# A linear-attention and expert kernel on one core: both heads' transposes and k-v products put into one stretch behind the third projection tile, and TensorE's order fixed in pairs 2 to 7

## Chip, cores and metric

The kernel runs on one core of one Trainium2 chip. The metric is the device time of one execution in microseconds (us), as a median over runs. All other times here are read from one profiled execution, and are counted from the start of its span. A "matmul" below is one TensorE instruction; a product of two unrounded fp32 tiles is two of them, a transpose is one.

## What is computed

The reference has three stages, and the change is in the first: an attention with random features, for 2 batches of 8 heads, 576 tokens and a head size of 64, with 128 features.

```python
def phi(x):
    proj = np.einsum('bhsd,md->bhsm', x, omega)
    sq = np.sum(x * x, axis=-1, keepdims=True) / 2.0
    h = proj - sq
    h = h - np.max(h, axis=-1, keepdims=True)
    return np.exp(h) / np.sqrt(m)
q_p, k_p = (phi(q_s), phi(k_s))
kv = np.einsum('bhsm,bhsd->bhmd', k_p, v)
z = np.sum(k_p, axis=2)
num = np.einsum('bhsm,bhmd->bhsd', q_p, kv)
den = np.einsum('bhsm,bhm->bhs', q_p, z)[..., None] + 1e-06
```

Behind it come a dense layer pair (`g = h * tanh(softplus(h))` between `x @ w_in` and `@ w_out`), and a top-1 mixture of 8 experts.

## The kernel before

The heads are taken in eight pairs (0 to 7). The loop over `i` at lines 407 to 445 has one round for each pair and one more. In round `i` the kernel projects pair `i` and finishes the pair before it, `a = i - 1`.

**Projection.** A pair's keys and queries are cut into tiles of 128 tokens: four tiles, and a fifth in odd pairs for the last 64 tokens of this pair and of the one before. `proj(i, t)` (line 246) makes one tile: six matmuls of rounded fp32 (two calls of `mm3`, whose three matmuls stand in lines 72, 73 and 74) into one PSUM bank of the tag "pj". There are three such banks, taken in turn, so a tile waits until the tile three before it in that tag has been read for the last time. (Tile 3 of pairs 0 and 1 lies in another bank, line 251.) Below, (2,2) is tile 2 of pair 2, its third.

**Features.** `phi(i, t)` (line 261) takes a tile out of its bank: VectorE finds the maximum of each row (line 266), ScalarE takes exponentials of the two key blocks (line 273), and the two query blocks are shifted, by ScalarE in even tiles (line 276, two instructions) and by VectorE in odd ones (line 271). Until then the bank is held.

**Finishing a pair.** For head `h` of pair `a`, `qtr(a, h)` (line 314) transposes the shifted query features (four transposes, line 322) and ScalarE takes their exponential into `qT` (line 323). `kvm(a, h)` (line 278) multiplies keys with v (eight matmuls, line 285, and in odd pairs two more for the last tokens, line 287). In odd pairs `qtr(a, 2)` does the last tokens' transposes (two, line 326), and `kvc` (line 305) copies z and kv out of PSUM, on ScalarE. `ratio` (line 336) begins with `heads`, the matmuls `den` and `num` (line 334, 8 and 16 of them), which need `qT`, `z` and `kv` of two pairs: `den` and `num` of the first token half are made in the round right behind the pair that completes them.

**Order.** `beat(i, t, *pe)` projects a tile, then runs the functions in `pe`, then traces `phi`. What stands in `pe` behind tiles 1, 2, 3 and 4 is the list `extra`, line 422:

```python
q = [(lambda h=h: qtr(a, h)) for h in range(3 if a % 2 else 2)]
kv = [(lambda h=h: kvm(a, h)) for h in range(2)] + [lambda: kvc(a // 2)] * (a % 2)
...
    extra = [q[0], kv[0]], [], [q[1], *kv[1:]], q[2:]
```

So head 0 stands behind tile 1 (the second), head 1 behind tile 3 (the fourth). This part of the program goes through a list scheduler at build time. It may place the instructions of an engine in another order than they are traced in, wherever data and buffers allow; `tc.issue_after(x)` keeps what is traced inside behind x on the same engine. The order on each engine is then fixed in the program. Behind this stage the order is as written (`manual_schedule`, line 472 on).

Of the kernel before, what the change touches and what calls it, by code (L numbers as in the profile page):

```python
# [22 lines left out]
NPAIR = NB * NH // 2  # L23
# [10 lines left out]
def performer_mish_moe(  # L34
# [16 lines left out]
    T, V, S, P = nc.tensor, nc.vector, nc.scalar, nc.gpsimd  # L51
# [13 lines left out]
    def split_hi_lo(src, hi, lo, eng_hi="act", eng_lo="pool"):  # L65

        round_hi(src, hi, eng_hi)
        take_lo(src, hi, lo, eng_lo)

    def mm3(o, lh, ll, rh, rl, start, stop):  # L70

        T.matmul(out=o, lhsT=lh, rhs=rh, start=start, stop=False)  # L72
        T.matmul(out=o, lhsT=lh, rhs=rl, start=False, stop=False)  # L73
        return T.matmul(out=o, lhsT=ll, rhs=rh, start=False, stop=stop)  # L74
# [4 lines left out]
    ident = cpool.tile([128, 128], F32, name="ident")  # L79
# [18 lines left out]
    def bank(tag, name):  # L98
        return psum.tile([128, 512], F32, name=name, tag=tag, bufs={"pj": 3, "qt": 2}.get(tag, 1))

    def twin(name):

        return psum.tile([128, 2, 512], F32, name=name, tag="b12", bufs=1)
# [60 lines left out]
    def advance(*gens):  # L164

        for x in gens:
            next(x, None)

    def finish(*gens):

        for x in gens:
            for _ in x:
                pass
# [18 lines left out]
    with ExitStack() as c2:  # L192
# [14 lines left out]
        V.tensor_scalar(out=omh, in0=omf, scalar1=SCALE, scalar2=None, op0=ALU.mult)  # L207
        V.scalar_tensor_tensor(out=oml, in0=omf, scalar=SCALE, in1=omh.bitcast(F32), op0=ALU.mult, op1=ALU.subtract)
        st = {}

        def pieces(p):
            cuts = {0: (0, 256, 768, 1024), 1: (0, 512, 1280)}.get(p, (0, 1280 if p % 2 else 1024))
            return [slice(*c) for c in zip(cuts, cuts[1:])]
# [12 lines left out]
        def vload(p):  # L228
            w = 780 if p % 2 else 520
            with tc.issue_after(st[2]["load"].ins) if p == 1 else ExitStack():  # L230
                nc.sync.dma_start(out=st[p]["v"][:, 0:w], in_=va[p][:, 0:w])

        def halves(p):

            return (("act", "dve"),) * 3 if p == 0 else (("pool", "pool"),) * 2 + (("dve", "pool"),) * 2 if p == 1 else (("pool", "pool"),) * 5

        def split(p):
            d = st[p]
            d["h"] = a3.tile([128, 1280], F32R, name="kqh", tag="kqh")
            d["l"] = a3.tile([128, 1280], F32R, name="kql", tag="kql")  # L240
            cut = pieces(p)[1:] if p == 0 else [slice(0, 256), slice(256, 512), slice(512, 768), slice(768, 1280)] if p == 1 else [slice(c, c + 256) for c in range(0, 1280 if p % 2 else 1024, 256)]
            for c, e in zip(cut, halves(p)):
                split_hi_lo(d["f"][:, c], d["h"][:, c], d["l"][:, c], *e)
                yield

        def proj(p, t):
            d = st[p]

            if (p, t) == (0, 3):
                st["twin"] = twin("pj")  # L250
            d["p", t] = ps = st["twin"][:, p, :] if t == 3 and p < 2 else bank("pj", "pj")
            for i in range(2):
                s = slice(256 * t + 128 * i, 256 * t + 128 * i + 128)
                if (p, t) == (0, 0):

                    T.matmul(out=ps[:, i * 256 : i * 256 + 256], lhsT=d["f"][:, s], rhs=oms, start=True, stop=True)
                    continue
                with tc.issue_after(st[0]["mm"].ins) if p == 0 and (t, i) > (1, 0) or p == 1 and t < 2 else ExitStack():
                    st[0]["mm"] = mm3(ps[:, i * 256 : i * 256 + 256], d["h"][:, s], d["l"][:, s], omh, oml, True, True)

        def phi(p, t):

# [15 lines left out]
        def kvm(p, h):  # L278

            d, du = st[p], st[p // 2, "u"]  # L280
            if p % 2 == 0 and h == 0:
                du["K"] = bank("b0", "kvp")
            e, v, K, c = d["e"], d["v"], du["K"], (2 * h + p % 2) * 65
            for t in range(4):
                T.matmul(out=K[:, c : c + 65], lhsT=e[t][:, h, :], rhs=v[:, (2 * t + h) * 65 : (2 * t + h + 1) * 65], start=(p % 2 == 0 and h == 0 and t == 0), stop=False)  # L285
            if p % 2:
                T.matmul(out=K[:, h * 130 : h * 130 + 130], lhsT=e[4][:, h, :], rhs=v[:, 520 + h * 130 : 650 + h * 130], start=False, stop=(h == 1))

        def lead(t):

# [23 lines left out]
        def qtr(p, h):  # L314
            e, d = st[p]["e"], st[p // 2, "u"]
            if p % 2 == 0 and h == 0:
                d["qT"] = a2.tile([128, 2, 2, SEQ], F32, name="qT", tag="qT")
            qT = d["qT"]
            q = bank("qt", "qt")
            if h < 2:  # L320
                for t in range(4):
                    T.transpose(q[:, t * 128 : t * 128 + 128], e[t][:, 2 + h, :], ident)  # L322
                S.activation(out=qT[:, p % 2, h, 0:512], in_=q, func=AF.Exp)
            else:
                for i in range(2):
                    T.transpose(q[:, i * 128 : i * 128 + 128], e[4][:, 2 + i, :], ident)
                S.activation(out=qT[:, :, :, 512:SEQ], in_=q[:, 0:256].rearrange("p (h r t) -> p r h t", h=2, r=2), func=AF.Exp)

        def heads(u, o, t0, w, s):

            d, n = st[u, "u"], o.shape[-1]
            for i in range(4):
                r, h = divmod(i, 2)
                T.matmul(out=o[32 * i : 32 * i + 32, :], lhsT=d[w][:, h, r, s], rhs=d["qT"][:, r, h, t0 : t0 + n], start=True, stop=True, tile_position=(0, 32 * i))  # L334

        def ratio(u, c, last=False):

# [68 lines left out]

        for i in range(NPAIR + 1):
            a, u, odd = i - 1, (i - 3) // 2, i % 2 == 1
            sp = split(i + 2) if i + 2 < NPAIR and i > 0 else iter(())
            advance(sp)  # L410
            if i == 1:
                lead(0)
            beat(i, 0, *([lambda: ratio(u, 1 - i % 2)] if u >= 0 else []))
            if i == 0:
                with tc.issue_after(st[0]["max"].ins):
                    finish(sp0)
            q = [(lambda h=h: qtr(a, h)) for h in range(3 if a % 2 else 2)]
            kv = [(lambda h=h: kvm(a, h)) for h in range(2)] + [lambda: kvc(a // 2)] * (a % 2)
            if i < 2:
                extra = [], [], [], []  # L420
            else:
                extra = [q[0], kv[0]], [], [q[1], *kv[1:]], q[2:]
            for t in range(4):
                if i == 0 and t > 1:
                    with tc.issue_after(st[0]["max"].ins):
                        advance(sp1)
                advance(sp)
                if i == 1 and t == 0:
                    lead(1)
                beat(i, t + 1, *extra[t])  # L430
                if i == 1 and t < 2:
                    lead(t + 2)
                if i == 0 and t == 3:
                    finish(sp1, split(2))
            finish(sp)
            if i + 3 < NPAIR:
                load(i + 3)
            if i + 2 < NPAIR:
                vload(i + 2)
            if i == 2:  # L440
                with tc.issue_after(st[4]["load"].ins):
                    nc.sync.dma_start(out=cs, in_=cst)
            with tc.issue_after(st[4]["load"].ins) if i == 2 else ExitStack():
                for x in loads.get(i, ()):
                    fetch(*x)
# [26 lines left out]
    with tc.manual_schedule():  # L472
# [116 lines left out]
        for k in range(4):  # L589
            s, now = 9 * k + 6, [3 * k + 1, 3 * k + 2, 3 * k + 3]  # L590
# [272 lines left out]
        for j in range(NJ):  # L863
# [4 lines left out]
            e = "pool" if j < 5 else "act"  # L868
# [68 lines left out]
        o = y2.tile([TT, 3, DM], F32, name="o", tag="o")  # L937
# [14 lines left out]
        o = y2.tile([TT, 3, DM], F32, name="o", tag="o")  # L952
# [33 lines left out]
    with tc.If(R["nrem"] > 0, label="rest"):  # L986
        with ExitStack() as c2:
# [5 lines left out]
            with tc.For_i(0, G, 1) as gi:  # L993
                ps = [*(bank("pj", "pq") for _ in range(3)), bank("b0", "pq")]
                for j in range(NJ):
                    t = q2.tile([128, 512], I64, name="wo64", tag="wo64")
                    nc.sync.dma_start(out=t, in_=w_out[j])
                    f = q2.tile([128, 512], F32, name="wof", tag="wof")
# [5 lines left out]
            with tc.For_i(0, G, 1) as gi:  # L1004
                with tc.For_i(0, E, 1) as ei:
                    n = nc.values_load(R["cnti"][0:1, ds(gi * E + ei, 1)], min_val=0, max_val=GT, skip_runtime_bounds_check_because="a count of a group's tokens")
                    with tc.If(n > 0):
# [7 lines left out]
                        w = q1.tile([TT, 3], F32, name="w", tag="w")  # L1015
# [7 lines left out]
                        for t in range(3):  # L1023
# [3 lines left out]
                            o = ob[:, ds(gi * 3 + t, 1), :].rearrange("p o d -> p (o d)")  # L1027
# [12 lines left out]
    with tc.manual_schedule():  # L1040
        yo3.append(cpool.tile([128, 4, 4, E], F32, name="yt2", tag="us", bufs=1).rearrange("p j q e -> p (j q e)")[:, 0:TT])
        pt = [bank("pj", "pt") for _ in range(3)]
        for t in range(3):
            c = slice(t * TT, t * TT + TT)
# [71 lines left out]
```

## Time and profile before

| | |
|---|---|
| median of 3 runs | 295.41 us (294.96 to 296.36) |
| the profiled execution | 294.71 us |
| its span, first to last instruction | 293.0 us |
| TensorE matmuls busy | 287.7 us, 98% |
| VectorE, ScalarE, GpSimd busy | 73%, 65%, 25% |
| granted TensorE clock, mean | 1.000 |

The span and the profiled execution's own time differ by what lies around the span, 1.71 us. A busy matmul row overlaps the next one, so busy time tells only that TensorE had something in hand; the distance between two starts tells what an instruction costs.

### The profile page before, as it was taken

To read this page: it belongs to the slowest core of one execution; us is meant where nothing else is said; L and a number is where in the kernel's file an instruction comes from. 1 tells how busy PE (TensorE), PEld (TensorE's weight loads), DVE (VectorE), ACT (ScalarE), POOL (GpSimd) and SP (SyncE) were. 2 spreads that over 40 slices of the span, in tenths; PEclk is the share of its full clock that TensorE was granted. 3 is DMA by queue.
4 is the path that set the end of the run, shared out by engine and by line. 5 is a ranking of instruction groups with operands and counts; after the bars stand their busy time and mean duration, and the time that the engine had idled before them with its cause. 6 is when DMAs were issued, how large, how long until landed. Compare 5 with 4: busy or idle time off the path is not lost.

```text
span 293.0 us, 6011 instructions
## 1 busy us (share of the span) xinstructions
PE 287.7 (98%) x2276; PEld 269.3 (92%) x2277; DVE 215.3 (73%) x392; ACT 189.9 (65%) x374; POOL 73.2 (25%) x110
## 2 busy tenths in 40 slices
PE   8999999999999999999999999999999999999994
PEld 5998988877999999999979997879999999999994
DVE  4766667997999999999898099958647764636621
ACT  4997787975294787978966989625446554435311
POOL 3899994232021101010021176300000000000000
PEclk9999999999999999999999999999999999999999
DMA  6767731230166579954610000000345508622011
GB/s 208 251 217 287 245 110 55 74 110 35 72 218 209 161 229 314 328 162 145 220 69 0 0 2 0 3 0 3 107 141 153 176 27 271 210 72 82 1 42 46
DMA packets 18433, 37.03 MB, mean 126 GB/s; under 512 B 1632, under 2 KB 7616, under 8 KB 18400
## 3 DMA queue, kind: packets, MB, share of 16 engines
q1 hardware_dynamic: 18256, 36.47, 38.0%
q8 instruction: 19, 0.31, 0.4%
q10 hardware_dynamic: 144, 0.13, 0.2%
q14 instruction: 14, 0.11, 0.1%
HBM read 33.06 MB, written 3.54 MB: 125 GB/s over the span
## 4 chain that ended last, share of the span: by engine, by line
PE 97%; DMA 1%; DVE 0%; ACT 0%; issue 0%
PE h L72 12%; PE h L74 11%; PE h L73 11%; PE py L72 9%; PE py L73 9%; PE py L74 9%; PE kvp L285 4%; PE pj L72 3%; PE pj L74 3%; PE ph L72 3%; PE ph L73 3%; PE ph L74 3%; PE pj L73 3%; PE num L334 3%; PE lg L532 3%; PE qt L322 2%
## 5 line engine op out<-in xcount | busy, mean ns | idle before, releaser
L72 PE MATMUL h<-xh,wih 128*128 128x384 f32 x192 | 64.7, 337 | 0.0
L74 PE MATMUL h<-xh,wil 128*128 128x384 f32 x192 | 64.3, 335 | 0.0
L73 PE MATMUL h<-xl,wih 128*128 128x384 f32 x192 | 64.2, 334 | 0.0
L72 PE MATMUL py<-gh,whi 128*128 128x288 f32 x128 | 38.4, 300 | 0.0
L63 DVE TENSOR_TENSOR wl<-wl,whi 128x512 fp32r<-128x512 f32 x48 | 33.9, 712 | 5.3 <-PE py L74 3.6
L73 PE MATMUL py<-gh,whi 128*128 128x288 f32 x128 | 37.6, 294 | 0.0
L74 PE MATMUL py<-gh,wl 128*128 128x288 f32 x128 | 37.5, 293 | 0.0
L72 PEld LDWEIGHTS h<-xh,wih 128*128 128x128 f32 x192 | 36.0, 188 | 1.1 <-issue 1.1
L73 PEld LDWEIGHTS h<-xl,wih 128*128 128x128 f32 x192 | 36.0, 188 | 0.0
L74 PEld LDWEIGHTS h<-xh,wil 128*128 128x128 f32 x192 | 36.0, 188 | 0.0
L266 DVE TENSOR_REDUCE nm<-pj 128x4 f32<-128x512 f32 x36 | 24.6, 687 | 13.7 <-PE pj L74 13.2
L482 ACT COPY g<-h 128x384 f32<-128x384 f32 x42 | 20.0, 477 | 21.2 <-PE h L74 21.1
L58 POOL TENSOR_SCALAR wih<-wif 128x512 fp32r<-128x512 f32 x13 | 11.2, 863 | 77.5 <-PE h L73 33.0
L526 DVE TENSOR_TENSOR g<-g,em 128x1152 f32<-128x1152 f32 x16 | 22.1, 1383 | 8.4 <-ACT em L524 8.4
L273 ACT ACTIVATE e<-pj,nm 128x128 f32<-128x128 f32 x72 | 22.7, 374 | 5.5 <-DVE nm L266 4.0
L72 PEld LDWEIGHTS py<-gh,whi 128*128 128x128 f32 x128 | 24.0, 188 | 1.3 <-POOL whi L58 0.6
L73 PEld LDWEIGHTS py<-gh,whi 128*128 128x128 f32 x128 | 24.1, 189 | 0.0
L74 PEld LDWEIGHTS py<-gh,wl 128*128 128x128 f32 x128 | 24.1, 188 | 0.0
L63 POOL TENSOR_TENSOR kql<-kqf,kqh 128x256 fp32r<-128x256 f32 (+1 forms) x31 | 22.9, 756 | 1.3 <-DVE kqh L60 1.0
L56 ACT CAST whi<-wl 128x512 fp32r<-128x512 f32 x39 | 23.2, 617 | 0.0
L63 DVE TENSOR_TENSOR gh<-g,gh 128x288 fp32r<-128x288 f32 x32 | 16.0, 506 | 9.7 <-ACT gh L56 9.1
L72 PE MATMUL pj<-omh,kqh 128*128 128x256 f32 x70 | 22.0, 314 | 0.0
(165 smaller groups left out, 700.6 us busy)
## 6 DMA issues: line engine op xcount, KB each, us to landing
wi<-w_in SPq DMA_DIRECT2D x16, 512.0 KB, 3.3
wo<-w_out SPq DMA_DIRECT2D x16, 512.0 KB, 4.0
wl<-w SPq DMA_DIRECT2D x32, 256.0 KB, 3.0
kqf<-kq SPq DMA_DIRECT2D x3, 640.0 KB, 3.8
out<-zero SPq DMA_DIRECT2D x4, 448.0 KB, 6.2
v<-va SPq DMA_DIRECT2D x4, 390.0 KB, 4.3
kqf<-kq SPq DMA_DIRECT2D x3, 512.0 KB, 4.1
v<-va SPq DMA_DIRECT2D x4, 260.0 KB, 4.9
```

The costliest lines, as they stand in the source:

```text
L56: S.copy(out=hi, in_=src)
L58: P.tensor_scalar(out=hi, in0=src, scalar1=1.0, scalar2=0.0, op0=ALU.mult, op1=ALU.add)
L63: (P if eng == "pool" else V).tensor_tensor(out=lo, in0=src, in1=hi.bitcast(F32), op=ALU.subtract)
L72: T.matmul(out=o, lhsT=lh, rhs=rh, start=start, stop=False)
L73: T.matmul(out=o, lhsT=lh, rhs=rl, start=False, stop=False)
L74: return T.matmul(out=o, lhsT=ll, rhs=rh, start=False, stop=stop)
L266: d["max"] = V.tensor_reduce(out=nm, in_=pv, op=ALU.max, axis=AX.X, negate=True)
L273: S.activation(out=e[:, j, :], in_=pv[:, j, :], func=AF.Exp, bias=nm[:, j : j + 1])
L285: T.matmul(out=K[:, c : c + 65], lhsT=e[t][:, h, :], rhs=v[:, (2 * t + h) * 65 : (2 * t + h + 1) * 65], start=(p % 2 == 0 and h == 0 and t ...
L334: T.matmul(out=o[32 * i : 32 * i + 32, :], lhsT=d[w][:, h, r, s], rhs=d["qT"][:, r, h, t0 : t0 + n], start=True, stop=True, tile_position= ...
L482: (S.copy if 2 < j or c == 2 else V.tensor_copy)(out=g(j, slice(c * 384, c * 384 + 384)), in_=ps)
L526: V.tensor_tensor(out=hv, in0=hv, in1=em.pop(j), op=ALU.mult)
```

## The change

Behind tile 2 (the third) of every round from 2 on stand now, in this order, the transposes of head 0, the products of head 0, those of head 1 (with `kvc` in odd pairs), and the transposes of head 1. The last tokens' transposes stay behind the last tile. In rounds 2 to 7 each TensorE instruction of the stage is issued behind the one traced before it, so that TensorE runs them as written. Nothing that is computed changes, and no instruction is added or taken away.

```diff
         st = {}
+        strict, last = [False], []
+
+        def follow():
+
+            return tc.issue_after(last[-1].ins) if strict[0] and last else ExitStack()
+
+        def mm(f, *args, **kw):
+
+            with follow():
+                last[:] = [f(*args, **kw)]
...
-                with tc.issue_after(st[0]["mm"].ins) if p == 0 and (t, i) > (1, 0) or p == 1 and t < 2 else ExitStack():
+                with tc.issue_after(st[0]["mm"].ins) if p == 0 and (t, i) > (1, 0) or p == 1 and t < 2 else follow():
                     st[0]["mm"] = mm3(ps[:, i * 256 : i * 256 + 256], d["h"][:, s], d["l"][:, s], omh, oml, True, True)
+                last[:] = [st[0]["mm"]]
...
-                T.matmul(out=K[:, c : c + 65], lhsT=e[t][:, h, :], rhs=v[:, (2 * t + h) * 65 : (2 * t + h + 1) * 65], start=(p % 2 == 0 and h == 0 and t == 0), stop=False)
+                mm(T.matmul, out=K[:, c : c + 65], lhsT=e[t][:, h, :], rhs=v[:, (2 * t + h) * 65 : (2 * t + h + 1) * 65], start=(p % 2 == 0 and h == 0 and t == 0), stop=False)
...
-                    T.transpose(q[:, t * 128 : t * 128 + 128], e[t][:, 2 + h, :], ident)
+                    mm(T.transpose, q[:, t * 128 : t * 128 + 128], e[t][:, 2 + h, :], ident)
...
         for i in range(NPAIR + 1):
             a, u, odd = i - 1, (i - 3) // 2, i % 2 == 1
+            strict[0] = 2 <= i < NPAIR
...
-                extra = [q[0], kv[0]], [], [q[1], *kv[1:]], q[2:]
+                extra = [], [q[0], *kv, q[1]], [], q[2:]
```

The matmuls of lines 287, 326 and 334 are wrapped in `mm` in the same way.

## Rows read from the trace of the kernel before

**Rows 1.** The page's busy time of TensorE, share of the span, instructions.

```profile
PE 287.7 (98%) x2276; PEld 269.3 (92%) x2277; DVE 215.3 (73%) x392; ACT 189.9 (65%) x374; POOL 73.2 (25%) x110
```

**Rows 2.** All waits of TensorE: total us, times, longest.

```profile
PE wp L204 <- PEq L1109: 1.0, 1, 1.0
PE pj L256 <- DVE oms L206: 0.4, 1, 0.4
PE pt L1047 <- ACT cs L1045: 0.3, 1, 0.3
```

**Rows 3.** Stretches: us, busy PE, PEld, DVE, ACT, POOL, clock, DMA.

```profile
15.80:21.34 5.54, 5.54 (x51) 5.41 (x49) 3.25 (x6) 5.53 (x21) 5.54 (x13) 1.00 0.77 239
...
44.51:53.39 8.88, 8.88 (x88) 7.83 (x87) 6.94 (x14) 6.76 (x23) 3.55 (x5) 1.00 0.21 66
53.39:61.50 8.11, 8.11 (x83) 7.03 (x82) 8.04 (x16) 6.48 (x19) 2.10 (x2) 1.00 0.29 108
```

**Rows 4.** Timeline of TensorE in round 2: start us, length us, instruction, count.

```profile
15.68 0.28 PE L74 MATMUL pj<-omh,kql 128*128 128x256 f32 x1
15.80 0.60 PE L322 MATMUL qt<-ident,e 128*128 128x128 f32 x4
...
17.27 0.37 PE L72 MATMUL pj<-omh,kqh 128*128 128x256 f32 x1
```

**Rows 5.** Timeline of VectorE ahead of it.

```profile
13.96 1.32 DVE L266 TENSOR_REDUCE nm<-pj 128x4 f32<-128x512 f32 x2 [0.75 <-PE pj L74]
```

**Rows 6.** Timeline of ScalarE at the same time.

```profile
15.32 1.15 ACT L273 ACTIVATE e<-pj,nm 128x128 f32<-128x128 f32 x4 [0.28 <-DVE nm L266]
16.34 0.65 ACT L276 ACTIVATE e<-pj,nm 128x128 f32<-128x128 f32 x2
```

**Rows 7.** Timeline of ScalarE near the end of the kernel.

```profile
288.56 0.24 ACT L1045 COPY cs<-py 128x96 f32<-128x96 f32 x1 [2.14 <-PE py L74]
```

**Rows 8.** Timeline of TensorE near the end of the kernel.

```profile
288.86 0.31 PE L1047 MATMUL pt<-ident,cs 128*96 128x128 f32 x1 [0.33 <-ACT cs L1045]
```

**Rows 9.** Timeline of TensorE: a head of an even pair, in round 3.

```profile
23.74 0.60 PE L322 MATMUL qt<-ident,e 128*128 128x128 f32 x4
24.18 1.00 PE L285 MATMUL kvp<-v,e 128*128 128x65 f32 x8
24.99 0.36 PE L72 MATMUL pj<-omh,kqh 128*128 128x256 f32 x1
25.19 0.28 PE L73 MATMUL pj<-oml,kqh 128*128 128x256 f32 x1
```

**Rows 10.** Timeline of TensorE: ten products in a row.

```profile
58.73 1.23 PE L285 MATMUL kvp<-v,e 128*128 128x65 f32 x10
59.76 0.37 PE L72 MATMUL pj<-omh,kqh 128*128 128x256 f32 x1
```

**Rows 11.** Timeline of TensorE: transposes followed by a projection tile.

```profile
18.06 0.38 PE L322 MATMUL qt<-ident,e 128*128 128x128 f32 x2
18.20 0.37 PE L72 MATMUL pj<-omh,kqh 128*128 128x256 f32 x1
18.40 0.28 PE L73 MATMUL pj<-oml,kqh 128*128 128x256 f32 x1
```

**Rows 12.** Timeline of TensorE: `den` and the tile behind `num`, in round 4.

```profile
28.61 0.69 PE L334 MATMUL den<-qT,z 128*32 128x288 f32 x8
...
30.20 0.38 PE L72 MATMUL pj<-omh,kqh 128*128 128x256 f32 x1
```

**Rows 13.** Timeline of TensorE: head 1's transposes in round 4.

```profile
34.68 0.60 PE L322 MATMUL qt<-ident,e 128*128 128x128 f32 x4
```

**Rows 14.** Timeline of ScalarE behind those transposes.

```profile
35.31 0.60 ACT L323 ACTIVATE qT<-qt 128x512 f32<-128x512 f32 x1 [1.09 <-PE qt L322]
...
36.81 0.30 ACT L311 COPY z<-kvp 128x128 f32<-128x128 f32 x1
...
37.22 0.69 ACT L273 ACTIVATE e<-pj,nm 128x128 f32<-128x128 f32 x2
```

More of the change, by code (lines that the diff above doesn't have):

```diff
@@ L284, in kvm @@
             for t in range(4):
-                T.matmul(out=K[:, c : c + 65], lhsT=e[t][:, h, :], rhs=v[:, (2 * t + h) * 65 : (2 * t + h + 1) * 65], start=(p % 2 == 0 and h == 0 and t == 0), stop=False)
+                mm(T.matmul, out=K[:, c : c + 65], lhsT=e[t][:, h, :], rhs=v[:, (2 * t + h) * 65 : (2 * t + h + 1) * 65], start=(p % 2 == 0 and h == 0 and t == 0), stop=False)
             if p % 2:
-                T.matmul(out=K[:, h * 130 : h * 130 + 130], lhsT=e[4][:, h, :], rhs=v[:, 520 + h * 130 : 650 + h * 130], start=False, stop=(h == 1))
+                mm(T.matmul, out=K[:, h * 130 : h * 130 + 130], lhsT=e[4][:, h, :], rhs=v[:, 520 + h * 130 : 650 + h * 130], start=False, stop=(h == 1))
         def lead(t):
@@ L325, in qtr @@
                 for i in range(2):
-                    T.transpose(q[:, i * 128 : i * 128 + 128], e[4][:, 2 + i, :], ident)
+                    mm(T.transpose, q[:, i * 128 : i * 128 + 128], e[4][:, 2 + i, :], ident)
                 S.activation(out=qT[:, :, :, 512:SEQ], in_=q[:, 0:256].rearrange("p (h r t) -> p r h t", h=2, r=2), func=AF.Exp)
@@ L333, in heads @@
                 r, h = divmod(i, 2)
-                T.matmul(out=o[32 * i : 32 * i + 32, :], lhsT=d[w][:, h, r, s], rhs=d["qT"][:, r, h, t0 : t0 + n], start=True, stop=True, tile_position=(0, 32 * i))
+                mm(T.matmul, out=o[32 * i : 32 * i + 32, :], lhsT=d[w][:, h, r, s], rhs=d["qT"][:, r, h, t0 : t0 + n], start=True, stop=True, tile_position=(0, 32 * i))
         def ratio(u, c, last=False):
```

## The prediction

> **What bounds the kernel now.** I read the page's busy times first: TensorE has work in hand for 98% of the span [rows 1]. Matmul rows overlap, so this alone does not tell that TensorE never waits. The list of all its waits does: three, 1.7 us together, at the start and the end, none in the attention [rows 2]. The table by stretches says the same of rounds 2, 6 and 7: TensorE is busy throughout, at a granted clock of 1.00, the level of 2.4 GHz [rows 3]. The reader is to see two things there. What TensorE executes or waits for in the attention goes straight into the total, for the dense layers behind it are TensorE's too and give nothing back. And other engines are close behind: ScalarE is busy 5.53 of 5.54 us in round 2, VectorE 8.04 of 8.11 us in round 7. The timelines of the engines then give the price of each step and, above all, when a buffer comes free.
>
> **Part 1: the work on TensorE.** No instruction goes or comes, so all that the grouping can save is the cost of changing from products to projection tiles and back. Take one head of an even pair [rows 9]: four transposes cost 0.44 us, eight products 0.81 to the start of the next tile, and from its first matmul to its second 0.20 pass, where two neighbours in a tile are about 0.12 apart (15.68 to 15.80 [rows 4]). So leaving products costs 0.08 us. Two more products in a row add 1.03 - 0.81 = 0.22 [rows 10], 0.11 each, so eight that stand behind other products cost 0.88, and 0.07 more than the eight that come fresh. Leaving transposes for a tile costs nothing: two and the first matmul take 0.34 [rows 11], and 2 x 0.11 + 0.12 is 0.34. The stretch of an even pair so saves two exits (0.16), gives back 0.07 and, for the last product before a transpose, some 0.03: 0.06 us. Where an odd pair's products end with those of line 287 I see no exit to save and put 0. Three even pairs (2, 4, 6) give 0.18 us; were odd pairs to save as much, 0.36. I take **-0.2 us**, bounds 0 and -0.4. The last tokens' two transposes only change neighbours: they now stand before `den` and no longer before a tile, at the same price.
>
> **Part 2: the fixed order, round 2.** The first three tiles of a round now stand together. Tiles (2,0) and (2,1) end in the old order with the matmul at 15.68; head 0's four transposes start at 15.80, and (2,2) only at 17.27 [rows 4]. In the new order (2,2) is due at 15.80. Which bank does it take? There are three in turn, and tile 3 of pair 1 lies elsewhere, so it is the bank of (1,4). That one is read by VectorE's maximum (the second of the two that start at 13.96 and end at 15.28 [rows 5]) and then by ScalarE. ScalarE takes four exponentials from 15.32, of (1,4) and (1,3), and then from 16.34 the two shifts, which can only be (1,4)'s, as odd tiles have none there: they end at 16.99 [rows 6]. Until then the bank is held. In the old order head 0's work covers this wait completely; the cover is gone, since head 0 is now queued behind (2,2) on TensorE, with head 1 and `den` behind it. ScalarE has no slack to deliver sooner [rows 3], and what it does up to there lies in rounds 0 and 1, which the change leaves alone.
>
> From the end of a ScalarE instruction to the first matmul that waits for it 0.06 us pass (288.56 + 0.24 = 288.80 [rows 7], 288.86 [rows 8]). So (2,2) starts at 16.99 + 0.06 = 17.05 and not at 15.80: 1.25 us. The first matmul behind a pause may cost up to 0.08 us more, as behind products. I take **+1.3 us**. The bounds: if ScalarE took the two shifts ahead of (1,3)'s two exponentials, the bank would be free 0.5 us earlier (16.34 - 15.32 over four, times two), which makes +0.75; +1.35 is the other end.
>
> Does anything behind it pay it back? Not on TensorE, which had no other wait to lose.
>
> No row of before has a matmul overtaking a waiting tile, and none could show it, because the old order has head 0 ahead of (2,2). The Trainium skill, TensorE: Matmul & The Clock Gate, Part 3, The mechanism, says that weight loads may be pulled ahead of matmuls in flight while matmuls themselves start and end strictly in order. By that rule the cover is gone and the sum stands at +1.1; were the queue able to let head 0's matmuls past the waiting tile, only part 1 would be left, -0.2.
>
> **Part 3: the same wait in rounds 4 and 6.** There the third tile takes the bank of (3,4) or (5,4). In round 2 the bank was held for 2.4 us from the start of its maximum (15.28 - 0.69 = 14.6, with 0.69 from 1.32 for two that overlap a little) to 16.99 [rows 5, 6], with ScalarE full. But between the two tiles now stand `den` and `num`, 30.20 - 28.61 = 1.59 us [rows 12], which they did not in round 2, and two tiles of 0.7 to 0.8 us: 3.0 us and more. I put 0; as an upper bound 0.1, were ScalarE as late as in round 2 and the maximum 0.7 us late. In odd rounds head 0's and head 1's work lies between as well.
>
> **Part 4: `den` behind the last tile.** In rounds 3, 5 and 7 `den` needs head 1's exponential, and head 1's transposes now come last in the stretch. From the first transpose to the end of the exponential the trace shows 35.31 + 0.60 - 34.68 = 1.23 us, with ScalarE idle before [rows 13, 14]; with the hand-over, 1.29. In the new order there lie between: the transposes (0.44, less the 0.08 by which the next tile starts early [rows 11]: 0.36), one tile of six matmuls (0.20 + 5 x 0.12 = 0.80), and the two last transposes with the step to `den` (about 0.31). That is 1.47 us, a margin of 0.18. The copies of z and kv hold ScalarE for 37.22 - 36.81 = 0.41 us [rows 14], but they are due when the products end, about 0.2 us into the transposes, and let the exponential start at 0.61, where the trace has 35.31 - 34.68 = 0.63. It just fits. I put 0, with the loss named below as a rival.
>
> VectorE and GpSimd do the same work and are moved past nothing; no DMA is moved, and the load that waits for a pair's v is freed a little sooner. That costs and gives nothing, as TensorE's own work covers it.
>
> **The sum.** 1.3 - 0.2 = +1.1 us. The profiled execution was 294.71 us with a span of 293.0; it would be 295.8 with 294.1. The median of the runs was 0.70 us above the profiled one, so I put the same 1.1 on it: 295.41 + 1.1 = **296.5 us**, +0.37%. A difference of 0.5% (1.48 us) is about what a measurement of this kernel can tell from no change.
>
> **Rivals.**
>
> *The wait in round 2 is hidden or short.* If (2,2) finds another bank, or ScalarE's order differs, from nothing to 0.75 us of the 1.3 remain: 295.2 to 296.0 us. Against it: the order of rounds 0 and 1 is not touched, and (2,0) and (2,1) hold the two other banks, filled last before 15.80 [rows 4]. This is also how the change would look if the order were fixed in name only. Chance 0.14.
>
> *A second wait, at `den`: slower than before.* The place is the step from rounds 2, 4 and 6 to the next. The scheduler may put the third tile's two exponentials and two shifts (16.34 - 15.32 = 1.02 us for four [rows 6]) on ScalarE ahead of head 1's exponential. The point from which it decides is the margin of 0.18 us; with all four ahead `den` is late by 1.02 - 0.18 = 0.84 us. Once makes 296.5 + 0.84 = 297.3 us, three times 299.0. For it: ScalarE is busy 6.76 of 8.88 us in round 6, and VectorE, which finds the maximum that they need, is nearly full from there [rows 3]. Against it: the third tile ends two heads' products and four transposes ahead of head 1's transposes, over 2 us (0.44 + 0.81 + 0.88 [rows 9, 10]), and its maximum and four activations are 0.7 + 1.0 us. Chance 0.24.
>
> *The grouping pays more than rows 9 to 11 show*, for instance because a better order in the last round, which is not fixed, saves splits of `den` and `num`. It would have to bring 2.6 us to end faster by over 0.5%; the waits of TensorE there are nil. Chance 0.04.
>
> My own forecast, one exposed wait and small savings, has 0.58.
>
> **Range and chances.** The likeliest case alone is 295.9 to 297.0. From the first rival the range takes in its lower end, -0.2 us: 295.2. From the second it takes the wait at one step, with its upper bound (1.35 - 0 + 0.84 = 2.2) 297.6, and leaves three such waits out. That holds about 0.58 + 0.14 + 0.11. Slower by over 0.5% (above 296.9): the second rival but its smallest waits, 0.20, and a tail of my own case, 0.08. Faster by over 0.5%: 0.04. The rest, 0.68, is no change that can be told.
>
> **What would show it.** In TensorE's waits a new row, a projection matmul (line 72) behind ScalarE's line 276, some 1.2 us, once, near 16 to 17 us. Round 2's (2,2) starts near 17.05, ScalarE's shifts still end near 17.0. In rounds 3 to 7 no wait of TensorE; an entry of `den` behind line 323 is the second rival, and no entry at all the first. From the first transpose of an even pair's stretch to the second matmul of the tile behind it some 2.7 us (0.44 + 0.81 + 0.88 + 0.03 + 0.36 + 0.20). The prediction is wrong if ScalarE's order ahead of 17 us has changed, or if waits in rounds 3 to 7 add up to more than half a microsecond.

## The result, and the profile after

The changed kernel takes 297.46 us (median of 10 runs, 296.45 to 298.61), the kernel before 295.42 in the same session: ratio 1.0064, 95% interval 1.0043 to 1.0085. The prediction was 296.5 us in a range of 295.2 to 297.6. The time lies in the range, near its upper end, and the forecast "no change that can be told" (up to 0.5%) is just missed. The profiled execution took 296.45 us with a span of 294.7 at a mean clock of 0.997.

The page's busy times are those of [rows 1], but for the span around them:

```profile
PE 287.9 (98%) x2276; PEld 269.2 (91%) x2277; DVE 214.7 (73%) x392; ACT 189.5 (64%) x374; POOL 73.3 (25%) x110
```

The work is the same and the span is 1.7 us longer, so TensorE waits more. The granted clock has no part in this: it is 1.00, the level of 2.4 GHz, in both traces up to 290 us, and the mean of 0.997 comes from the last stretch, where TensorE has little left to do (us, busy PE, PEld, DVE, ACT, POOL, clock, DMA):

```profile
290.00:294.70 4.70, 0.90 (x6) 0.43 (x4) 0.63 (x2) 0.89 (x4) 0.00 (x0) 0.81 0.15 35
```

TensorE's list of waits shows where it waits (compare [rows 2]; line 1121 was 1109, 266 was 256, 1059 was 1047):

```profile
PE pj L72 <- POOL kqh L58: 1.1, 1, 1.1
PE wp L204 <- PEq L1121: 1.0, 1, 1.0
PE pj L266 <- DVE oms L206: 0.5, 1, 0.5
PE pj L72 <- DVE den L366: 0.5, 1, 0.5
PE pt L1059 <- ACT cs L1057: 0.3, 1, 0.3
```

Two rows are new, both at line 72, the first matmul of a projection tile, once 1.1 and once 0.5 us. The releasers named (the instructions whose end is taken for the end of the wait) are GpSimd's line 58 and VectorE's line 366, a step of the ratio. Both names are wrong, as the timelines and the experiments show. In the timelines below line 219 is the helper `mm`, through which the transposes, the products, `den` and `num` now go; lines 277, 282, 322 and 366 were 266, 271, 311 and 355.

**Wait 1, tile (2,2).** TensorE's timeline in round 2 (compare [rows 4]):

```profile
15.47 0.27 PE L74 MATMUL pj<-omh,kql 128*128 128x256 f32 x1
16.88 0.36 PE L72 MATMUL pj<-omh,kqh 128*128 128x256 f32 x1 [1.13 <-POOL kqh L58]
17.07 0.28 PE L73 MATMUL pj<-oml,kqh 128*128 128x256 f32 x1
...
17.67 0.60 PE L219 MATMUL qt<-ident,e 128*128 128x128 f32 x4
```

ScalarE's and GpSimd's at the same time (line 284 was 273, line 287 was 276):

```profile
15.63 0.63 ACT L284 ACTIVATE e<-pj,nm 128x128 f32<-128x128 f32 x2
16.13 0.64 ACT L287 ACTIVATE e<-pj,nm 128x128 f32<-128x128 f32 x2
```

```profile
15.99 0.76 POOL L58 TENSOR_SCALAR kqh<-kqf 128x256 fp32r<-128x256 f32 x2
```

Tile (2,2) was due 0.12 behind the matmul at 15.47, at 15.59, and starts at 16.88: 1.29 us late. Its second matmul comes 0.19 later where neighbours are 0.12 apart: 0.07 more, so the wait costs 1.36 us. ScalarE's two shifts of (1,4) end at 16.77, 0.11 ahead of the start. GpSimd's rounding of the next pair ends at 16.75, and that is all that its name in the wait rests on. Head 0's transposes, which stood ahead of (2,2) in [rows 4], come at 17.67.

**Wait 2, tile (7,2).** Timelines of TensorE, VectorE and ScalarE:

```profile
56.46 0.28 PE L74 MATMUL pj<-omh,kql 128*128 128x256 f32 x1
57.21 0.36 PE L72 MATMUL pj<-omh,kqh 128*128 128x256 f32 x1 [0.47 <-DVE den L366]
57.40 0.28 PE L73 MATMUL pj<-oml,kqh 128*128 128x256 f32 x1
```

```profile
53.37 0.69 DVE L277 TENSOR_REDUCE nm<-pj 128x4 f32<-128x512 f32 x1
54.83 1.28 DVE L63 TENSOR_TENSOR wil<-wif,wih 128x512 fp32r<-128x512 f32 x1 [0.78 <-ACT wih L56]
56.03 0.41 DVE L282 TENSOR_TENSOR e<-pj,nm 128x256 f32<-128x256 f32 x1
...
56.70 0.45 DVE L366 SCALAR_TENSOR_TENSOR den<-den,r 128x288 f32<-128x288 f32 x1
```

```profile
54.15 0.65 ACT L56 CAST wih<-wif 128x512 fp32r<-128x512 f32 x1
...
56.48 0.63 ACT L284 ACTIVATE e<-pj,nm 128x128 f32<-128x128 f32 x2 [0.52 <-DVE e L282]
```

By the same reckoning: due at 56.58, start 57.21, 0.63 late, and 0.07 for the restart: 0.70 us. Tile (7,2) takes the bank of (6,3), an odd tile: VectorE finds its maximum (line 277) and shifts its queries (line 282), ScalarE takes its exponentials. Between maximum and shift VectorE now has line 63, a subtraction for a weight of the dense layer, which waits 0.78 us for ScalarE's cast and then takes 1.28. The shift comes at 56.03 and the exponentials end at 57.11, 0.10 ahead of the tile. In the trace of before VectorE did the shift first:

```profile
53.36 0.41 DVE L271 TENSOR_TENSOR e<-pj,nm 128x256 f32<-128x256 f32 x1
53.84 1.43 DVE L63 TENSOR_TENSOR wil<-wif,wih 128x512 fp32r<-128x512 f32 x1
```

The diff does not touch this code; the scheduler placed VectorE's instructions anew. It is the new grouping that brings this, not the fixed order: e4_free, with the grouping alone, has the subtraction first as well, and e5_order, with the fixed order alone, has the shift first (both below). Why the scheduler chose so the trace does not tell.

**What was saved.** The stretch of an even pair (compare [rows 9]):

```profile
25.60 0.60 PE L219 MATMUL qt<-ident,e 128*128 128x128 f32 x4
...
27.77 0.60 PE L219 MATMUL qt<-ident,e 128*128 128x128 f32 x4
28.13 0.36 PE L72 MATMUL pj<-omh,kqh 128*128 128x256 f32 x1
28.33 0.28 PE L73 MATMUL pj<-oml,kqh 128*128 128x256 f32 x1
```

From the first transpose to the second matmul of the tile pass 2.73 us. Over two rounds, an odd and an even pair, `den` of round 4 to `den` of round 6 took 44.51 - 28.61 = 15.90 us in before and takes 45.54 - 29.70 = 15.84 now: 0.06 saved, 0.18 for three such steps. The step ahead of it bears this out: from the last product of round 1 to `den` of round 4 it is 1.30 us more than in before (28.61 - 12.82 and 29.70 - 12.62), which is wait 1 less 0.06. The third step was not measured, since the last round runs in another order.

**The ledger.** One stretch holds all of it: from the last product of round 1 (12.82 us in before, 12.62 after) to the last matmul of `num` (70.57 and 72.34). It takes 57.75 us in before and 59.73 after, 1.98 more. From there to the last matmul of the first dense layer every trace of this study shows 103.78 or 103.79 us: nothing is given back behind the attention. The terms are 1.36 + 0.70 - 0.18 = 1.88. The other 0.10 lie in the last round, whose order is not fixed: from the first product behind (7,2) (58.42) to the last matmul of `num` the changed kernel takes 13.92 us, and e2_shift (below), where the scheduler ordered this round otherwise, 13.75.

### The profile page after: what moved, and what is told of

It reads as the page before. It is cut to its first block, busy times and chain, and to the rows that moved or that the text cites. A ratio compares the mean times of both kernels' runs of the same rounds, so it can differ in the third digit from the quotient of the medians.

```text
span 294.7 us, 6018 instructions
## 1 busy us (share of the span) xinstructions
PE 287.9 (98%) x2276; PEld 269.2 (91%) x2277; DVE 214.7 (73%) x392; ACT 189.5 (64%) x374; POOL 73.3 (25%) x110
## 4 chain that ended last, share of the span: by engine, by line
PE 95%; ACT 1%; DMA 1%; DVE 1%; issue 1%; POOL 0%; POOLq 0%
PE h L72 12%; PE h L73 11%; PE h L74 11%; PE py L72 9%; PE py L73 9%; PE py L74 9%; PE kvp L219 5%; PE pj L72 3%; PE ph L72 3%; PE ph L74 3%; PE ph L73 3%; PE lg L544 3%; PE pj L73 3%; PE pj L74 3%; PE num L219 2%; PE qt L219 2%
```

## The experiments

Seven kernels, each in 5 rounds beside the kernel before. "Stretch" is the one of the ledger; the waits are from the start of one matmul to the next, 0.12 where there is none. Both are taken from starts that are not rounded, so their last digit can differ by 0.01 from the rows.

| kernel | ratio (95%) | stretch us | wait at (2,2) | wait at (7,2) |
|---|---|---|---|---|
| before | 1 | 57.75 | none | none |
| after | 1.0064 (1.0043 to 1.0085) | 59.73 | 1.40 | 0.75 |
| e1_bank | 1.0073 (1.0046 to 1.0099) | 59.52 | 0.88 | 1.05 |
| e2_shift | 1.0048 (1.0028 to 1.0068) | 58.89 | 1.40 | none |
| e3_both | 1.0018 (1.0000 to 1.0035) | 58.42 | 0.89 | none |
| e4_free | 1.0018 (0.9997 to 1.0039) | 58.04 | none | 0.28, behind a transpose |
| e5_order | 1.0051 (1.0029 to 1.0072) | 59.11 | none | none |
| e6_second | 0.9991 (0.9971 to 1.0012) | 57.73 | none | none |
| e7_from3 | 1.0004 (0.9983 to 1.0026) | 57.60 | none | none |

**e1_bank: another bank for (2,2).** Edits are against the changed kernel.

```diff
-            d["p", t] = ps = st["twin"][:, p, :] if t == 3 and p < 2 else bank("pj", "pj")
+            d["p", t] = ps = st["twin"][:, p % 2, :] if t == 3 and p < 2 or (p, t) == (2, 2) else bank("pj", "pj")
```

> Changed kernel, but tile (2,2) lies in the free half of the double bank that held tile 3 of pair 0, so that it need not wait for the bank of (1,4); TensorE's order stays. If the wait in round 2 is for ScalarE's two shifts of (1,4), it is gone: the 1.41 us between the starts at 15.47 and 16.88 fall to 0.12, the time falls by about 1.36 us to 296.1 us, some +0.25% on the kernel before. If it is for GpSimd's rounding of keys, which the profile names as releaser, the wait and the time stay (297.5 us).

Timelines of TensorE, ScalarE and GpSimd in round 2:

```profile
15.37 0.27 PE L74 MATMUL pj<-omh,kql 128*128 128x256 f32 x1
16.25 0.36 PE L72 MATMUL pj<-omh,kqh 128*128 128x256 f32 x1 [0.61 <-POOL kql L63]
```

```profile
15.01 1.15 ACT L284 ACTIVATE e<-pj,nm 128x128 f32<-128x128 f32 x4
16.03 0.64 ACT L287 ACTIVATE e<-pj,nm 128x128 f32<-128x128 f32 x2
```

```profile
16.32 0.78 POOL L58 TENSOR_SCALAR kqh<-kqf 128x256 fp32r<-128x256 f32 x2
```

The wait falls to 0.88 and does not vanish. Tile (2,2) now starts before the shifts end (16.67), and even before GpSimd's line 58 starts: neither holds it any more, and GpSimd never did. What it follows is the four exponentials, by 0.09 us (15.01 + 1.15 = 16.16). Two of them read tile (1,3), which lies in the other half of the double bank. So the wait goes with the last reader of whatever bank the tile is given. The expectation, that the wait would be gone altogether, had overlooked these readers.

The stretch gains only 0.21 us, which the ratio cannot tell from nothing, because wait 2 grew. Timeline of TensorE in round 7:

```profile
55.83 0.28 PE L74 MATMUL pj<-omh,kql 128*128 128x256 f32 x1
56.88 0.36 PE L72 MATMUL pj<-omh,kqh 128*128 128x256 f32 x1 [0.78 <-DVE den L366]
```

TensorE comes to (7,2) 0.63 us earlier than in the changed kernel, but the tile can start only 0.33 earlier: part of what the first wait gave was lost again at the second.

**e2_shift: in round 6 the conversion is issued behind the shift.**

```diff
-                    with tc.issue_after(st[i]["max"].ins):
+                    with tc.issue_after(st[i]["shift" if (i, t) == (6, 3) else "max"].ins):
                         advance(conv)
```

> Changed kernel, but the conversion step behind tile (6,3) is issued on VectorE behind the shift of (6,3) and no longer ahead of it. If the wait of (7,2) in round 7 is for the bank of (6,3), held because that shift stands behind a subtraction that itself waits for ScalarE, the wait of 0.63 us goes and the time falls by about 0.7 us to 296.75 us. If it is for VectorE's first step on den (line 366), which the profile names and which here comes some 2 us later in VectorE's order, the wait grows by a microsecond or more (298.5 us). The wait in round 2 stays either way.

Timelines of TensorE, VectorE and ScalarE:

```profile
56.08 0.28 PE L74 MATMUL pj<-omh,kql 128*128 128x256 f32 x1
56.20 0.34 PE L72 MATMUL pj<-omh,kqh 128*128 128x256 f32 x1
```

```profile
53.71 0.42 DVE L282 TENSOR_TENSOR e<-pj,nm 128x256 f32<-128x256 f32 x1
54.45 1.28 DVE L63 TENSOR_TENSOR wil<-wif,wih 128x512 fp32r<-128x512 f32 x1 [0.31 <-ACT wih L56]
```

```profile
55.48 0.61 ACT L284 ACTIVATE e<-pj,nm 128x128 f32<-128x128 f32 x2
```

The shift comes at 53.71 in place of 56.03, and wait 2 is gone; wait 1 stays at 1.40. The stretch is 0.84 us shorter than in the changed kernel, where 0.70 was expected of this wait alone: from `den` of round 7 to the first product behind (7,2) it is 0.64 less (53.48 to 58.42, here 53.10 to 57.40), and behind that product 0.17, because the edit also changed the scheduler's order of the last round. The exponentials of (6,3) end at 56.09, 0.11 ahead of the tile, so the bank comes free only just in time. So the order of VectorE's queue is the cause of wait 2, not line 366 that the list names.

**e3_both: the edits of e1_bank and e2_shift together.**

> Both edits together. If the two waits are independent and are all that the change costs, both are gone and the time is that of the kernel before, 295.4 us, less about 0.2 for the grouping and plus about 0.1 for the last round (ratio 0.999 to 1.001). If a stall that is taken away only moves elsewhere, a new wait of TensorE of 0.5 us or more shows in rounds 3 to 7 and the ratio stays above 1.002.

One wait is left in the attention, the 0.89 at (2,2), and the stretch is 58.42: 1.31 less than the changed kernel. Apart the edits gave 0.21 and 0.84; together they give 0.26 more than that sum, since the time won at (2,2) is no longer lost again at (7,2).

**e4_free: the new grouping, no fixed order.**

```diff
-            strict[0] = 2 <= i < NPAIR
+            strict[0] = False
```

> The new grouping with TensorE's order left to the planner. The planner then puts head 0's transposes and products with v of round 2 between the tiles (2,1) and (2,2), and part of num of round 7 between the tiles (7,0) and (7,1). Theory (grouping is worth -0.18 us up to round 7, and the loss is the two waits for banks of the products, 1.36 and 0.70 us, which the order written out lays open): neither of the two waits is seen, the span is 292.7 to 293.1 us and the ratio to the kernel before 0.998 to 1.000. Rival (the grouping itself costs the time, by what the single stretch does to the readers of the banks): the span stays within 0.4 us of the changed kernel's 294.7 and the ratio at 1.005 or more.

Neither wait is in the list, and the span is 292.9 us, as the theory has it; but the ratio came out at 1.0018, a little above its range, and the stretch is 0.29 us over before. The ratio cannot be told from 1, and the rival's 1.005 is out. All of the excess lies behind `den` of round 6: from there to the last `num` e4_free takes 26.49 us, before and e7_from3 (below) 26.06. Timelines of VectorE, ScalarE and TensorE in round 7:

```profile
52.99 1.28 DVE L63 TENSOR_TENSOR wil<-wif,wih 128x512 fp32r<-128x512 f32 x1 [0.77 <-ACT wih L56]
54.19 0.41 DVE L282 TENSOR_TENSOR e<-pj,nm 128x256 f32<-128x256 f32 x1
```

```profile
54.64 0.62 ACT L284 ACTIVATE e<-pj,nm 128x128 f32<-128x128 f32 x2 [0.53 <-DVE e L282]
```

```profile
55.08 0.27 PE L219 MATMUL qt<-ident,e 128*128 128x128 f32 x1
55.36 0.36 PE L72 MATMUL pj<-omh,kqh 128*128 128x256 f32 x1
```

The subtraction stands ahead of the shift here too, though TensorE's order is free. Tile (7,2) starts 0.10 us behind the exponentials of (6,3) (54.64 + 0.62 = 55.26) and 0.28 behind the start of a transpose, which takes 0.11 in a row of four: wait 2 is still there, for the most part filled with other work. The scheduler moved three matmuls of tile (7,0) between `den` and `num` and one transpose ahead of (7,2). From `den` of round 7 to the last matmul of tile (7,1) it is 3.32 us (51.64 to 54.96) and in e7_from3 2.99 (51.76 to 54.75), so the split of `den` and `num` costs 0.33. From there to the first product behind (7,2) it is 1.51 us (to 56.47) and 1.33 (to 56.08): 0.18 more, by what is left of the wait. Behind that product 0.09 come back.

**e5_order: the old places, with the fixed order.**

```diff
-                extra = [], [q[0], *kv, q[1]], [], q[2:]
+                extra = [q[0], kv[0]], [], [q[1], *kv[1:]], q[2:]
```

> The old places of the transposes and products with v, with the order of pairs 2 to 7 fixed as written. Theory: the wait of tile (2,2) for its bank is gone, since head 0's work stands ahead of it; but den now stands directly behind the copies' inputs at the end of rounds 3, 5 and 7, which the planner had kept apart by two products, so that TensorE waits there some 0.4 to 0.5 us each time; nothing is won by grouping. Span 293.0 + 3 x 0.45 = 294.3 us, ratio 1.003 to 1.006. Rival (only the grouping makes waits, the fixed order by itself costs nothing): no wait in the attention over 0.3 us, span 293.0 us, ratio 0.999 to 1.001.

No wait at (2,2), but two rows of 0.5 us at `den`, and the span is 294.7. Timelines of TensorE and ScalarE in round 5:

```profile
36.88 0.38 PE L219 MATMUL qt<-ident,e 128*128 128x128 f32 x2
37.80 0.69 PE L219 MATMUL den<-qT,z 128*32 128x288 f32 x8 [0.54 <-ACT z L322]
```

```profile
36.46 0.62 ACT L284 ACTIVATE e<-pj,nm 128x128 f32<-128x128 f32 x2
36.96 0.64 ACT L287 ACTIVATE e<-pj,nm 128x128 f32<-128x128 f32 x2
37.46 0.29 ACT L322 COPY z<-kvp 128x128 f32<-128x128 f32 x1
```

`den` follows the copy of z by 0.05 us (37.46 + 0.29 = 37.75), and the copy stands behind four activations of the tile. From the second transpose to `den` it is 0.81 us here and in round 7 and 0.41 in round 3, where the changed kernel has 0.20: 0.61 + 0.61 + 0.21 = 1.43, nearly all of the stretch's +1.36. So the fixed order costs time by itself, at another place than in the changed kernel. It is the order that the scheduler was free to choose that hid these waits in before. VectorE's shift of (6,3) stands ahead of the subtraction in this kernel, as in before:

```profile
54.62 0.41 DVE L282 TENSOR_TENSOR e<-pj,nm 128x256 f32<-128x256 f32 x1
55.09 1.44 DVE L63 TENSOR_TENSOR wil<-wif,wih 128x512 fp32r<-128x512 f32 x1
```

**e6_second: the stretch of both heads behind the second tile, order fixed.**

```diff
-                extra = [], [q[0], *kv, q[1]], [], q[2:]
+                extra = [q[0], *kv, q[1]], [], [], q[2:]
```

> Changed kernel, but the stretch stands behind the second tile (tile 1) of each round and not behind the third; TensorE's order stays fixed as written. If what costs is that the third tile comes before its bank is free, the stretch of 2.7 to 3.2 us covers both waits again: none in rounds 2 to 7, 295.2 us, ratio to before 0.998 to 1.001. If a fixed order costs by itself, wherever the stretch stands, waits appear in other places and the ratio stays near 1.005.

TensorE has no wait in the attention: both heads' transposes and products stand ahead of (2,2) and (7,2). At (2,2) they cover the wait for the bank. At (7,2) the run does not test this, because VectorE does the shift of (6,3) at 54.56 here, ahead of the subtraction at 54.89. The ratio is 0.9991 (0.9971 to 1.0012). Grouping and fixed order cost nothing measurable when the stretch stands one tile earlier.

**e7_from3: fixed order from round 3 on, with the edit of e2_shift.**

```diff
-            strict[0] = 2 <= i < NPAIR
+            strict[0] = 3 <= i < NPAIR
```

> The new grouping, fixed order from round 3 on only, and VectorE's conversion of round 6 issued behind that tile's shift instead of its maximum. Theory: wait 1 is hidden by the planner's own order of round 2, wait 2 by the shift's place; what is left is the grouping's -0.18 us and the last round's +0.09: span 292.8 to 293.1 us, ratio 0.998 to 1.000. Rival (something else than the two waits makes the changed kernel longer): span 293.4 us or more, ratio 1.002 or more.

TensorE in round 2:

```profile
15.14 0.28 PE L74 MATMUL pj<-omh,kql 128*128 128x256 f32 x1
15.26 0.60 PE L219 MATMUL qt<-ident,e 128*128 128x128 f32 x4
15.69 1.28 PE L219 MATMUL kvp<-v,e 128*128 128x65 f32 x10
16.73 0.36 PE L72 MATMUL pj<-omh,kqh 128*128 128x256 f32 x1
```

Left free, the scheduler puts head 0 ahead of (2,2) again, as in [rows 4]; no wait is left, and the stretch is 0.15 us shorter than in before. Head 0's work was ready at 15.26: only its place in the queue keeps it from filling wait 1 in the changed kernel. No version is measurably faster than the kernel before: 0.15 us is 0.05%.

## Why the prediction held, and where not

- **The number.** The measured 297.46 us lies in the range, but in part by luck. The likeliest case alone ended at 297.0; the range reached 297.6 because it took in a wait at `den`, which did not come. A sign of being wrong that the prediction named itself, waits in rounds 3 to 7 of more than half a microsecond, is met by the starts (0.63 us at (7,2)) and just not by the list (0.47).
- **Part 1 held.** 0.06 us for an even pair, 2.7 us for its stretch: measured 0.06 for two rounds and 2.73. The sum -0.2 is -0.18, if the step that was not measured is like the others.
- **Part 2 held.** The place, the bank of (1,4), and the price: 1.25 us late and up to 0.08 for the restart were put down, 1.29 and 0.07 came. The start at 17.05 is 16.88, since the whole of round 2 lies 0.21 us earlier in this execution and ScalarE's shifts with it. The hand-over took 0.11 us and not 0.06. In the prediction's list of signs the row of waits should have named ScalarE's shift; it named an instruction of GpSimd that ended within 0.02 us of it. The trace agrees with the rule of the Trainium skill, TensorE: Matmul & The Clock Gate, Part 3, The mechanism, that matmuls start in program order: the transposes that run at 15.26 in e7_from3 stand at 17.67 behind the waiting tile.
- **Part 3 failed.** The step is its last sentence, that in odd rounds the heads' work lies between as well, and so 0. It does not: the stretch stands ahead of a pair's fourth tile, and between (6,3) and (7,2) there are only two transposes, `den`, `num` and two tiles, as in even rounds. What went with it is the sentence behind part 4 that VectorE is moved past nothing. Its code is unchanged, its order is not. Where the margin in rounds 4 and 6 holds, in round 7 the subtraction in front of the shift takes it: 0.70 us. And the margin was smaller than part 3 had it: with the shift first (e2_shift) the bank is free just 0.11 us before the tile starts. The Trainium skill, PSUM — Partial Sum Buffer, Engine vs sequencer instructions, says that VectorE's queue is strictly first in, first out. The trace agrees: the shift had its maximum at 54.06, and stood behind the subtraction until 56.03.
- **Part 4 held.** From the last tokens' transposes to `den` it is 0.31 or 0.32 us in rounds 3, 5 and 7, no wait. The margin of 0.18 us was enough. Lines of round 3:

```profile
21.49 0.38 PE L219 MATMUL qt<-ident,e 128*128 128x128 f32 x2
21.80 0.69 PE L219 MATMUL den<-qT,z 128*32 128x288 f32 x8
```

- **The rivals.** The second one, another exposed wait, came about in kind and size (0.70 for 0.84 us) but at another place and by another engine's queue. e5_order shows its place, `den` behind ScalarE's activations, in the old grouping. The first (a hidden or short wait in round 2) and the third (grouping pays 2.6 us) did not come: 1.29 us late, and about 0.18 saved. The sum of the prediction, +1.1 us, lacks mainly this wait: with 0.70 it is 1.8, and the medians differ by 2.04. Without wait 2 (e2_shift) the ratio is 1.0048, on the side of the 0.5% that was forecast.

## What to carry to other kernels

A planner's order that looks arbitrary may be what hides the release of a buffer: before fixing an order by hand, list for every tile which bank it takes, who reads that bank last, and what stands between. Do this again for the engines that the change does not name, since new places for one engine's instructions can make the planner choose anew on the others, as they did on VectorE here. When one wait is taken away, look at the next one on the same engine in the same trace: it may take part of the gain back.

## What the runs showed that was not expected

- The releaser that the list of waits names was wrong for both new waits (GpSimd's line 58, VectorE's line 366); each had only ended 0.06 to 0.13 us before the start (57.15 for 57.21, 16.75 for 16.88). Where a tile waits for a bank, the readers of that bank are the ones to look up.
- In e1_bank, tile (2,2) is written into the half of the double bank that only (0,3) had used before, and yet starts 0.09 us behind exponentials that read the other half: the two halves were given free together. Whether the program or the chip ties them the run does not tell.
- At both waits the first matmul behind the pause is 0.19 us ahead of the second, not 0.12: each pause costs 0.07 us more than its length. No long pause is needed for this: in e2_shift (7,2) starts on time and its second matmul still comes 0.18 behind. At (7,2) of the changed kernel the weight load of the first matmul starts at 57.18, 0.03 us ahead of it, where that of the matmul before started 0.11 ahead (56.35 for 56.46). That the late load is the cause is not shown.
